# Where the D/2 row joins the first layer: VectorE's addition or ScalarE's write ahead of the products

## The chip, the cores and the metric

The kernel runs on one core of a Trainium2 chip. Its time is the device time of one launch in microseconds (us); the median of repeated runs is what is compared. Before the change it is 1832.67 us, the median of three runs (1832.33 to 1833.54).

## The reference

A two-dimensional Fourier transform of eight sequences, of which the real part is kept, followed by a hard-swish MLP on every token:

```
X = np.fft.fft(x, axis=1)             # x: (8, 3008, 256)
X = np.fft.fft(X, axis=2)
x = X.real.reshape(8 * 3008, 256)
h = x @ w_in                          # (256, 2048)
g = h * np.clip(h + 3.0, 0.0, 6.0) / 6.0
out = g @ w_out                       # (2048, 256)
```

## The kernel before

The transform along the sequence is done in two stages of matmuls (47 and 64 points) per pair of sequences; the transform along the 256 columns is folded into `w_in` once, which gives the table `W1`. What the first layer reads is `q`: the cosine half (block 0) and the sine half (block 1) of the columns, 128 rows each. The last row of block 1 isn't a sine: it is the column D/2. Its values, spread over all partitions, stand in `qn`, and its row of `W1`, turned into a column, in `WN`; so `qn * WN[:, f]` is what that row gives to 128 units of the hidden layer.

A *chunk* is 256 columns of `q` (one chunk in twelve, the last of a pair, has 194). There are 4 pairs of sequences, 12 chunks in a pair, and 8 steps (`fc`) in a chunk, each for 256 of the 2048 hidden units: 384 steps, `s`. From step 22 (`SPLIT`) on every step is one *cycle* of the main loop (L1394 on), which works on three chunks' steps at once:

- `odd_half` of step s+2: six TensorE products with the sine half (`half_products`, block 1) into the PSUM banks `u` and `v` in which the cosine half already lies; then ScalarE copies `v` to `y` (L669), VectorE joins it to `u` (L670), and ScalarE applies the first ReLU, `t<-u` (L708).
- `mlp2` of step s: seven products of the second layer (fourteen TensorE instructions, L758) into the four banks `acc`, from the gated values `a` and their sums `c`, which GpSimd makes (`combine`, L725).
- `even_half` of step s+3: six products with the cosine half (block 0) into the other pair of banks `u`, `v`. These six and the other six are in the split number format: three tables `KW[:, j]` by three parts `k[:, j]`, j = 0 and 1 into `u`, j = 2 into `v`.
- `add_row` of step s+3 (L653): two VectorE instructions, `d = qn * WN + v`. Then `keep_even` (L660), `s = u * (1 + EPS) + d`, the whole cosine half with the D/2 row.
- `other_sign` of step s+2 (L679), `v = u - 2 * s`, and its ReLU `t<-v`; then `first_gate` and `second_gate` (L711), which write `a`.

Both signs are needed, since a column and its mirrored one differ in the sign of the cosine half. In `odd_half` the last of the 128 rows of block 1 is the D/2 row, so that `u` takes it from the product there, and `s` takes it from `add_row`.

There are four such banks (`a0`, `a1`, `y0`, `y1`): the two of an even step and the two of an odd one. Some cycles *lend* them: where a stage of the transform of later data is due (`behind`, `middle_fns`), it takes the banks of step s+3 for itself after `mlp2`'s first product and before `even_half`; there `n` is 3, the order of the products is (0, 1, 2), and `add_row` and `keep_even` come after `first_gate`. In the other cycles `n` is 1: one second-layer product stands between `odd_half` and `even_half` and six behind it, and the order is (2, 0, 1), `v` first. In the last step of a chunk (`closes`) all of `mlp2` is issued before the rest, and ScalarE copies the four banks `acc` out to `e` (`copy_sums`, L775), two in that cycle, two in the next.

Every engine takes its instructions in the order in which the program issues them; the engines wait for each other through semaphores that the tile framework sets by the tiles that are read and written. The tiles `y`, `t` and `d` have one buffer each, `s` two.

Of the kernel before, what the change touches and what calls it, by code (L numbers as in the profile page):

```python
# [7 lines left out]
F32 = mybir.dt.float32  # L8
# [7 lines left out]
AF = mybir.ActivationFunctionType  # L16
# [44 lines left out]
def kernel(  # L61
# [10 lines left out]
    nc = tc.nc  # L72
    P = nc.NUM_PARTITIONS
# [16 lines left out]
    TB = KC * N2  # L90
# [20 lines left out]
    ps_u = ctx.enter_context(tc.tile_pool(name="ps_u", bufs=1, space=PSUM))  # L111
# [428 lines left out]
    class Chunk:  # L540
# [3 lines left out]
        def __init__(self, pr, ck):  # L544
            self.pr, self.ck = pr, ck
            self.last = ck == NCK - 1
            self.first = ck == 0 and pr.p == 0
            self.final = self.last and pr.p == NP - 1
            self.ns = 3 if self.last else KC
            self.n = self.ns * N2  # L550
            self.nq = P + 2 * NH if self.last else TB
            self.a, self.c, self.acc, self.front, self.k = {}, {}, {}, {}, None
            k1 = [(ck * KK + j // 2 + 1) % NK1 for j in range(KC)]
            b = [j % 2 for j in range(KC)]
            if pr.p == 0 and ck < 2 * NSG:
                k1 = [ck % NSG * KC + j + 1 for j in range(KC)]
                b = [ck // NSG] * KC
            self.blocks = [[(2 * b[j] + h, (k1[j], N1 - k1[j])[m]) for j in range(KC) for h in range(2)]
                           for m in range(2)]
            if self.last:  # L560
                for m in range(2):
                    self.blocks[m][4:] = [(m, 0), (2 + m, 0)]
# [68 lines left out]

        return others

    def half_products(ch, fc, blk, u, v, order=(2, 0, 1)):
        nq = ch.nq
        for j in order:
            for i in range(2):
                fs = slice((2 * fc + i) * P, (2 * fc + i + 1) * P)
                nc.tensor.matmul((u, u, v)[j][:, i, 0:nq], KW[:, j, blk, fs], ch.k[:, j, blk, 0:nq],  # L639
                                 start=(blk == i == 0 and j != 1), stop=True, skip_group_check=True)  # L640

    def even_half(ch, fc, step, order):
        u = ps_u.tile([P, 2, TB], F32, tag=f"a{step % 2}", name="u")
        v = ps_u.tile([P, 2, TB], F32, tag=f"y{step % 2}", name="v")
        half_products(ch, fc, 0, u, v, order)
        ch.front[fc] = [u, v]

    def add_row(ch, fc):
        of, nq, qn, (u, v) = ch.ck % 2 * TB, ch.nq, ch.pr.qn[ch.ck // 2], ch.front[fc]
        d = spool.tile([P, 2, TB], F32, tag="d", bufs=1, name="d")  # L650
        for i in range(2):
            f = 2 * fc + i
            nc.vector.scalar_tensor_tensor(d[:, i, 0:nq], qn[:, of:of + nq], WN[:, f:f + 1], v[:, i, 0:nq],  # L653
                                           op0=AL.mult, op1=AL.add)
        ch.front[fc].append(d)
# [4 lines left out]
        nc.vector.scalar_tensor_tensor(s[:, :, 0:nq], u[:, :, 0:nq], 1.0 + EPS, d[:, :, 0:nq], op0=AL.mult, op1=AL.add)  # L660
        ch.front[fc] = [u, v, s]

    def odd_half(ch, fc):
        nq, (u, v, s) = ch.nq, ch.front[fc]
        half_products(ch, fc, 1, u, v)
        y = spool.tile([P, 2, TB], F32, tag="y", bufs=1, name="y")
        t = spool.tile([P, 2, 2, TB], F32, tag="t", bufs=1, name="t")
        un, vn, yn, tn = u[:, :, 0:nq], v[:, :, 0:nq], y[:, :, 0:nq], t[:, :, :, 0:nq]
        nc.scalar.copy(yn, vn)  # L669
        nc.vector.scalar_tensor_tensor(un, un, 1.0 + EPS, yn, op0=AL.mult, op1=AL.add)  # L670
        copy_sums(1)
        relu(tn[:, 0], un, 1.0 / 6.0)
        copy_sums(1)
        ch.front[fc] = [u, v, t, s]
# [8 lines left out]
    def first_gate(ch, fc):  # L683
        u, v, t = ch.front[fc]
        a = apool.tile([P, 2, 2, TB], F32, tag="a", name="a")
        ch.a[fc] = a
        if not ch.last:
            gate(a[:, 0], t[:, 0], u[:])
            return
        gate(a[:, 0, :, 0:P], t[:, 0, :, 0:P], u[:, :, 0:P])  # L690
        for f in range(2):
            gate(slots(a[:, 0, f], N2 // 2, 1), *(slots(x, NH, 1)[:, :, 0:NH - 1] for x in (t[:, 0, f], u[:, f])))
# [492 lines left out]
    def chunk(s):  # L1185
        p, ck, fc = steps[s]
        return chunks[p][ck], fc
# [155 lines left out]
    for s, (p, ck, fc) in enumerate(steps):  # L1343
        now[0] = s
        if ck == 0 and fc == 0:
            ahead, behind, middle_fns = beside(p)
            if p + 1 < NP:
                feed.work.append(fold_pieces(pairs[p + 1]))
        t = ck * NF + fc
        if t == NST * (NG - 1) + 2:  # L1350
            assert not feed.work and not pieces, (s, len(feed.work), len(pieces))
        run(ahead, t)
        if s < NF:

            (second_steps if s % 2 else first_steps)(s)

            for part in LATER.get(s, ()):
                for dst, src in later[part]:
                    nc.sync.dma_start(out=dst, in_=src)
            run(middle_fns, t)  # L1360

        else:
            if pieces and pieces[0][0] <= s and t not in middle_fns and t not in behind:
                behind[t] = [(stage1, pieces.pop(0)[1:])]

            def sums():
# [12 lines left out]
                feed.cycle(cost, (4.75 if s < SPLIT else 4.44) + 0.9 * (t in middle_fns) + 1.2 * (t in behind))  # L1379

            if s < SPLIT:
                run(middle_fns, t)
                others = split_w(SPLIT_W.index(s)) if s in SPLIT_W else None
                activate(*chunk(s + 2), *mlp1_products(*chunk(s + 2)), between=others)
                sums()
                mlp2(*chunk(s), 0, 3)
                if s == SPLIT - 1:
                    even_half(*chunk(s + 3), s + 3, (2, 0, 1))
                    add_row(*chunk(s + 3))
                    keep_even(*chunk(s + 3))  # L1390
                stage1_parts(t)
                mlp2(*chunk(s), 3, 7)
                copy_sums(4)
            else:  # L1394
                turn_of[0] = s + 3
                borrows = t in behind or t in middle_fns
                n = 3 if borrows or s == SPLIT else 1
                odd, even = s + 2 < len(steps), s + 3 < len(steps)
                if s == SPLIT:
                    mlp2(*chunk(s), 0, n)  # L1400
                if odd:
                    odd_half(*chunk(s + 2))
                if s > SPLIT:
                    mlp2(*chunk(s), 0, 1)
                stage1_parts(t)
                run(middle_fns, t)
                if s > SPLIT and n > 1:
                    mlp2(*chunk(s), 1, n)
                if even:
                    even_half(*chunk(s + 3), s + 3, (0, 1, 2) if borrows else (2, 0, 1))  # L1410
                closes = fc == NF - 1
                if closes:
                    mlp2(*chunk(s), n, 7)
                    copy_sums(1)
                if even and not borrows:
                    add_row(*chunk(s + 3))
                if odd:
                    other_sign(*chunk(s + 2))
                if closes:
                    copy_sums(1)  # L1420
                if even and not borrows:
                    keep_even(*chunk(s + 3))
                if odd:
                    first_gate(*chunk(s + 2))
                if even and borrows:
                    add_row(*chunk(s + 3))
                    keep_even(*chunk(s + 3))
                if odd:
                    second_gate(*chunk(s + 2))
                sums()  # L1430
                if not closes:
                    mlp2(*chunk(s), n, 7)
                elif s + 1 == len(steps):
                    copy_sums(4)
        if fc == NF - 1:
            prev = chunks[p][ck]
# [102 lines left out]
```

## Time and profile before

| | |
|---|---|
| median of three runs | 1832.67 us |
| the profiled execution's own time | 1833.52 us |
| its span in the profile | 1831.7 us |
| granted TensorE clock | 0.997 |
| TensorE matmuls busy | 1816.0 us, 99% |
| VectorE busy | 1622.5 us, 89% |
| GpSimd busy | 1529.5 us, 83% |
| ScalarE busy | 962.7 us, 53% |

In the profile PE is TensorE, PEld its weight loads, DVE VectorE, ACT ScalarE, POOL GpSimd. A row of the timeline has the start of an instruction in us from the span's start, its duration, the engine, the line, the operation, the tile that it writes and those that it reads, and the shape; at its end, in brackets, the idle time of the engine before it and what ended it. Neighbouring instructions of one kind are merged (x4), and one in fp32 is two matmul instructions. Matmuls are pipelined: the start of one that follows another format is recorded before it streams, so that rates are read from start to start over a whole cycle.

### The profile page before, as it was taken

Reading aid. Unit: us, or ns where it says so; the run is one execution under the profiler, and the core shown is the slowest. Engines: PE = TensorE matmul, PEld = TensorE weight load, DVE = VectorE, ACT = ScalarE, POOL = GpSimd, SP = SyncE. Lnnn points to the kernel's source line nnn. Section 1 sums busy time; section 2 is a strip of 40 time slices with the busy share of each in tenths; the row PEclk is TensorE's granted clock in tenths of the full one; section 3 lists DMA queues with packets and bytes.
Section 4 is the critical chain, followed back from the end, with each engine's and each line's share of the span. In section 5 each row is a group of like instructions: output and inputs, shape, how many; then the busy total and the mean of one; then the engine's idle time right before and its main releaser. Section 6 shows DMA issues by size and latency. Waiting matters only on the chain.

```text
span 1831.7 us, 32501 instructions
## 1 busy us (share of the span) xinstructions
PE 1816.0 (99%) x10896; PEld 1620.8 (88%) x10896; DVE 1622.5 (89%) x3132; ACT 962.7 (53%) x1630; POOL 1529.5 (83%) x1694
## 2 busy tenths in 40 slices
PE   9999999999999999999999999999999999999997
PEld 6688888889998888899999888889999999999997
DVE  8978888888998888888998888888989989999897
ACT  6554555555455555554555555555554555555553
POOL 5687999998789999987778999998777778777884
PEclk9999999999999999999999999999999999999999
DMA  8433232321122313111122232310111111102001
GB/s 272 117 95 93 78 102 60 74 61 41 44 61 78 88 41 93 41 48 29 30 61 64 62 83 58 87 50 23 36 39 30 45 30 30 41 18 47 18 14 31
DMA packets 157629, 110.54 MB, mean 60 GB/s; under 512 B 121952, under 2 KB 136090, under 8 KB 157462
## 3 DMA queue, kind: packets, MB, share of 16 engines
q1 hardware_dynamic: 148710, 82.22, 18.0%
q0 software_dynamic: 7504, 25.65, 4.6%
q8 instruction: 87, 1.43, 0.3%
q10 hardware_dynamic: 1248, 0.59, 0.1%
q14 instruction: 80, 0.66, 0.1%
HBM read 71.93 MB, written 36.79 MB: 59 GB/s over the span
## 4 chain that ended last, share of the span: by engine, by line
PE 91%; DVE 5%; DMA 2%; ACT 1%; issue 1%; SPq 0%; ACTq 0%; DVEq 0%
PE acc L758 58%; PE u L639 18%; PE v L639 9%; PE ps L526 2%; PE ps L296 1%; DVE a L711 1%; PE v L577 1%; PE u L577 1%; PE acc L735 1%; DVE d L653 1%; DVE s L660 0%; DVE u L670 0%; DVE s L586 0%; ACT t L708 0%; DMA xt<-in_x_dram,IT 0%
## 5 line engine op out<-in xcount | busy, mean ns | idle before, releaser
L758 PE MATMUL acc<-c,G 128*128 128x256 f32 (+1 forms) x3008 | 697.4, 375 | 0.0
L758 PEld LDWEIGHTS acc<-c,G 128*128 128x128 f32 x3008 | 559.9, 190 | 70.1 <-POOL c L725 2.4
L758 PE MATMUL acc<-a,G 128*128 128x256 f32 (+1 forms) x2256 | 599.7, 376 | 0.0
L725 POOL TENSOR_TENSOR c<-a 128x512 f32<-128x512 f32 (+1 forms) x375 | 471.8, 1258 | 128.2 <-DVE a L711 111.7
L639 PE MATMUL u<-k,KW 128*128 128x256 f32 (+1 forms) x2880 | 468.6, 285 | 0.4 <-DVE s L660 0.2
L708 ACT ACTIVATE t<-u,half 128x512 f32<-128x512 f32 (+1 forms) x384 | 260.6, 679 | 309.1 <-DVE u L670 253.5
L758 PEld LDWEIGHTS acc<-a,G 128*128 128x128 f32 x2256 | 372.9, 189 | 37.3 <-issue 17.6
L639 PE MATMUL v<-k,KW 128*128 128x256 f32 (+1 forms) x1440 | 403.0, 361 | 0.7 <-DVE a L711 0.7
L639 PEld LDWEIGHTS u<-k,KW 128*128 128x128 f32 x2880 | 393.5, 189 | 5.9 <-ACT z L306 1.0
L669 ACT COPY y<-v 128x512 f32<-128x512 f32 (+1 forms) x360 | 207.7, 577 | 320.8 <-PE v L639 320.8
L708 ACT ACTIVATE t<-v,half 128x512 f32<-128x512 f32 (+1 forms) x384 | 260.3, 678 | 201.2 <-DVE v L679 200.5
L670 DVE SCALAR_TENSOR_TENSOR u<-u,y 128x512 f32<-128x512 f32 (+1 forms) x360 | 247.1, 686 | 110.5 <-ACT y L669 94.2
L653 DVE SCALAR_TENSOR_TENSOR d<-qn,WN,v 128x256 f32<-128x256 f32 (+1 forms) x720 | 307.2, 468 | 9.9 <-PE v L639 9.6
L639 PEld LDWEIGHTS v<-k,KW 128*128 128x128 f32 x1440 | 265.1, 189 | 35.9 <-PE u L639 1.5
L725 POOL TENSOR_TENSOR c<-a,c 128x256 f32<-128x256 f32 (+1 forms) x375 | 269.5, 719 | 29.4
L725 POOL TENSOR_TENSOR c<-c,a 128x256 f32<-128x256 f32 (+1 forms) x375 | 269.1, 718 | 29.4
L679 DVE SCALAR_TENSOR_TENSOR v<-s,u 128x512 f32<-128x512 f32 (+1 forms) x360 | 246.4, 684 | 51.9 <-ACT t L708 51.3
L711 DVE SCALAR_TENSOR_TENSOR a<-t,u 128x512 f32<-128x512 f32 (+2 forms) x448 | 260.4, 593 | 3.2 <-ACT t L708 3.2
L711 DVE SCALAR_TENSOR_TENSOR a<-t,v 128x512 f32<-128x512 f32 (+1 forms) x480 | 263.2, 565 | 0.1
L660 DVE SCALAR_TENSOR_TENSOR s<-u,d 128x512 f32<-128x512 f32 (+1 forms) x360 | 242.6, 674 | 2.5
L725 POOL TENSOR_TENSOR e<-e 128x512 f32<-128x512 f32 (+2 forms) x184 | 182.8, 994 | 0.0
L775 ACT ACTIVATE e<-acc 128x512 f32<-128x512 f32 (+2 forms) x184 | 98.6, 537 | 4.7 <-PE acc L758 4.2
(140 smaller groups left out, 1093.1 us busy)
## 6 DMA issues: line engine op xcount, KB each, us to landing
out_dram<-o SPq DMA_DIRECT2D x744, 32.0 KB
T<-in_c_stage_dram SPq DMA_DIRECT2D x26, 512.0 KB
g<-zd SPq DMA_DIRECT2D x42, 256.0 KB
zd<-z SPq DMA_DIRECT2D x48, 192.0 KB
xt<-in_x_dram SPq DMA_DIRECT2D x21, 256.0 KB
qn<-qd SPq DMA_DIRECT2D x16, 256.0 KB
st<-in_moe_w_out_dram POOLq DMA_DIRECT2D x7, 512.0 KB, 6.2
xt<-in_x_dram SPq DMA_DIRECT2D x17, 192.0 KB
```

What stands on the lines that cost most here:

```text
L526: nc.tensor.matmul(ps[:, blk, u * P:n].rearrange("p (b k) -> p b k", b=2), g[:, kk, blk * (P + 1):blk * (P + 1) + P], T[gr][:, :, blk, kk, ...
L639: nc.tensor.matmul((u, u, v)[j][:, i, 0:nq], KW[:, j, blk, fs], ch.k[:, j, blk, 0:nq], start=(blk == i == 0 and j != 1), stop=True, skip_g ...
L653: nc.vector.scalar_tensor_tensor(d[:, i, 0:nq], qn[:, of:of + nq], WN[:, f:f + 1], v[:, i, 0:nq], op0=AL.mult, op1=AL.add)
L660: nc.vector.scalar_tensor_tensor(s[:, :, 0:nq], u[:, :, 0:nq], 1.0 + EPS, d[:, :, 0:nq], op0=AL.mult, op1=AL.add)
L669: nc.scalar.copy(yn, vn)
L670: nc.vector.scalar_tensor_tensor(un, un, 1.0 + EPS, yn, op0=AL.mult, op1=AL.add)
L679: nc.vector.scalar_tensor_tensor(vn, sn, -2.0, un, op0=AL.mult, op1=AL.add)
L708: nc.scalar.activation(t, h, AF.Relu, bias=half[:], scale=scale)
L711: nc.vector.scalar_tensor_tensor(dst, t, 1.0, h, op0=AL.min, op1=AL.mult)
L725: (eng or nc.gpsimd).tensor_tensor(out, in0, in1, op=AL.add)
L758: nc.tensor.matmul(ch.acc[i // 2][:, i % 2, 0:ch.n], G[:, i, fc, :], mv, start=(fc == 0 and i % 2 == 0), stop=(fc == NF - 1), skip_group_c ...
L775: nc.scalar.mul(e, acc, 1.0 / WS)
```

## The change

In a cycle that lends no bank, and in which the bank's last user wrote its full width (`written`), ScalarE writes `qn * WN` into the bank `v` of step s+3 ahead of the cosine half's products (`seed_row`, two instructions behind the copy to `y`). The products for `v` then start without clearing the bank's marks, so that they add to what stands there, and come last (order (0, 1, 2)); three second-layer products stand ahead of them instead of one. `add_row` becomes a ScalarE copy of `v` to `d`, ahead of `other_sign`; `keep_even` moves behind `first_gate`. The products of the sine half take 127 rows in place of 128 for such a step, since `v` has the D/2 row already.

```diff
-    def half_products(ch, fc, blk, u, v, order=(2, 0, 1)):
+    def half_products(ch, fc, blk, u, v, order=(2, 0, 1), seeded=False):
...
-                nc.tensor.matmul((u, u, v)[j][:, i, 0:nq], KW[:, j, blk, fs], ch.k[:, j, blk, 0:nq],
-                                 start=(blk == i == 0 and j != 1), stop=True, skip_group_check=True)
+                nc.tensor.matmul((u, u, v)[j][:, i, 0:nq], KW[0:P - (blk and seeded), j, blk, fs],
+                                 ch.k[0:P - (blk and seeded), j, blk, 0:nq],
+                                 start=(blk == i == 0 and j == 0) or (blk == i == 0 and j == 2 and not seeded),
+                                 stop=True, skip_group_check=True)
...
+    def seed_row(ch, fc, step):
...
+        ch.front[fc] = [u, v]
+        of, nq, qn = ch.ck % 2 * TB, ch.nq, ch.pr.qn[ch.ck // 2]
+        for i in range(2):
+            f = 2 * fc + i
+            nc.scalar.activation(v[:, i, 0:nq], qn[:, of:of + nq], AF.Identity, scale=WN[:, f:f + 1])
...
+    def even_half(ch, fc, step, order):
+        seeded = fc in ch.front
+        if not seeded:
...
+            written[step % 2] = ch.nq == TB
+        half_products(ch, fc, 0, *ch.front[fc], order, seeded)
+        ch.seeded[fc] = seeded
...
     def add_row(ch, fc):
...
+        if ch.seeded[fc]:
+            nc.scalar.copy(d[:, :, 0:nq], v[:, :, 0:nq])
+            ch.front[fc].append(d)
+            return
...
-    def odd_half(ch, fc):
+    def odd_half(ch, fc, between=None):
...
-        half_products(ch, fc, 1, u, v)
+        half_products(ch, fc, 1, u, v, seeded=ch.seeded[fc])
...
         nc.scalar.copy(yn, vn)
+        if between:
+            between()
...
-                n = 3 if borrows or s == SPLIT else 1
                 odd, even = s + 2 < len(steps), s + 3 < len(steps)
+                seeds = even and not borrows and written.get(turn_of[0] % 2)
+                n = 3 if borrows or seeds or s == SPLIT else 1
...
+                if borrows:
+                    written[turn_of[0] % 2] = False
                 if odd:
-                    odd_half(*chunk(s + 2))
+                    odd_half(*chunk(s + 2), (lambda: seed_row(*chunk(s + 3), s + 3)) if seeds else None)
...
-                    even_half(*chunk(s + 3), s + 3, (0, 1, 2) if borrows else (2, 0, 1))
+                    even_half(*chunk(s + 3), s + 3, (0, 1, 2) if borrows or seeds else (2, 0, 1))
...
-                if even and not borrows:
+                if even and not borrows and not seeds:
                     keep_even(*chunk(s + 3))
                 if odd:
                     first_gate(*chunk(s + 2))
+                if even and seeds:
+                    keep_even(*chunk(s + 3))
```

More of the change, by code (lines that the diff above doesn't have):

```diff
@@ L551, in __init__ @@
             self.nq = P + 2 * NH if self.last else TB
-            self.a, self.c, self.acc, self.front, self.k = {}, {}, {}, {}, None
+            self.a, self.c, self.acc, self.front, self.seeded, self.k = {}, {}, {}, {}, {}, None
             k1 = [(ck * KK + j // 2 + 1) % NK1 for j in range(KC)]
@@ L638, in half_products @@
                 fs = slice((2 * fc + i) * P, (2 * fc + i + 1) * P)
-                nc.tensor.matmul((u, u, v)[j][:, i, 0:nq], KW[:, j, blk, fs], ch.k[:, j, blk, 0:nq],
-                                 start=(blk == i == 0 and j != 1), stop=True, skip_group_check=True)
-    def even_half(ch, fc, step, order):
+                nc.tensor.matmul((u, u, v)[j][:, i, 0:nq], KW[0:P - (blk and seeded), j, blk, fs],
+                                 ch.k[0:P - (blk and seeded), j, blk, 0:nq],
+                                 start=(blk == i == 0 and j == 0) or (blk == i == 0 and j == 2 and not seeded),
+                                 stop=True, skip_group_check=True)
+    written = {}
+    def seed_row(ch, fc, step):
         u = ps_u.tile([P, 2, TB], F32, tag=f"a{step % 2}", name="u")
         v = ps_u.tile([P, 2, TB], F32, tag=f"y{step % 2}", name="v")
-        half_products(ch, fc, 0, u, v, order)
         ch.front[fc] = [u, v]
+        of, nq, qn = ch.ck % 2 * TB, ch.nq, ch.pr.qn[ch.ck // 2]
[5 more added lines that the diff above has]
+        if not seeded:
+            u = ps_u.tile([P, 2, TB], F32, tag=f"a{step % 2}", name="u")
+            v = ps_u.tile([P, 2, TB], F32, tag=f"y{step % 2}", name="v")
+            ch.front[fc] = [u, v]
+            written[step % 2] = ch.nq == TB
+        half_products(ch, fc, 0, *ch.front[fc], order, seeded)
+        ch.seeded[fc] = seeded
     def add_row(ch, fc):
```

## The prediction

> **What bounds the kernel now.** I read the page first, then busy time by stretches, then the timeline of single cycles, then the groups by shape.
>
> ```profile
> span 1831.7 us, 32501 instructions
> PE 1816.0 (99%) x10896; PEld 1620.8 (88%) x10896; DVE 1622.5 (89%) x3132; ACT 962.7 (53%) x1630; POOL 1529.5 (83%) x1694
> ...
> PE 91%; DVE 5%; DMA 2%; ACT 1%; issue 1%; SPq 0%; ACTq 0%; DVEq 0%
> ...
> 600.00:900.00 300.00, 300.00 (x1800) 269.11 (x1799) 265.94 (x480) 159.33 (x269) 265.57 (x288) 1.00 0.22 55
> ```
>
> TensorE is busy all the time, and the chain of waits lies on it for 91%. The busy share alone proves little, since the ends of matmuls are modelled. So the question is whether a cycle lasts as long as its products stream, or longer. One full cycle that lends no bank, from the sine half's first product to the next one's:
>
> ```profile
> 903.51 0.59 PE L639 MATMUL v<-k,KW 128*128 128x256 f32 x2
> 904.19 0.59 ACT L669 COPY y<-v 128x512 f32<-128x512 f32 x1 [0.95 <-PE v L639]
> 904.65 0.59 PE L639 MATMUL v<-k,KW 128*128 128x256 f32 x2
> 904.81 0.70 DVE L670 SCALAR_TENSOR_TENSOR u<-u,y 128x512 f32<-128x512 f32 x1
> 905.42 0.86 DVE L653 SCALAR_TENSOR_TENSOR d<-qn,WN,v 128x256 f32<-128x256 f32 x2
> 905.54 0.69 ACT L708 ACTIVATE t<-u,half 128x512 f32<-128x512 f32 x1 [0.77 <-DVE u L670]
> 905.56 1.02 PE L758 MATMUL acc<-a,G 128*128 128x256 f32 x4
> 906.26 0.70 DVE L679 SCALAR_TENSOR_TENSOR v<-s,u 128x512 f32<-128x512 f32 x1
> 906.42 1.89 PE L758 MATMUL acc<-c,G 128*128 128x256 f32 x8
> 906.87 0.68 DVE L660 SCALAR_TENSOR_TENSOR s<-u,d 128x512 f32<-128x512 f32 x1
> 907.96 0.59 PE L639 MATMUL v<-k,KW 128*128 128x256 f32 x2
> 908.07 0.68 DVE L711 SCALAR_TENSOR_TENSOR a<-t,v 128x512 f32<-128x512 f32 x1
> 908.38 0.63 PE L639 MATMUL u<-k,KW 128*128 128x256 f32 x4
> ```
>
> The cycle takes 4.45 us, and its 26 matmul instructions have no gap. VectorE runs behind but in time: `s`, which the next sine half's products into `u` must find done, ends at 907.55, and those start at 908.38, 0.83 later. In these cycles the row's addition (0.86 us on VectorE) lies beside TensorE and costs nothing.
>
> Where there is something to gain is a pair's last chunk, whose products are shorter while VectorE's work shrinks less:
>
> ```profile
> 475.23 0.55 PE L639 MATMUL v<-k,KW 128*128 128x194 f32 x2
> 479.60 0.55 PE L639 MATMUL v<-k,KW 128*128 128x194 f32 x2
> ...
> 506.61 0.53 PE L639 MATMUL v<-k,KW 128*128 128x256 f32 x2
> 506.87 0.62 ACT L612 ACTIVATE k<-q 128x512 fp32r<-128x512 f32 x1
> 508.19 0.48 PE L639 MATMUL v<-k,KW 128*128 128x256 f32 x2 [0.23 <-DVE a L711]
> 510.79 0.53 PE L639 MATMUL v<-k,KW 128*128 128x256 f32 x2
> 515.49 0.59 PE L639 MATMUL v<-k,KW 128*128 128x256 f32 x2
> ...
> 1802.59 0.50 PE L639 MATMUL v<-k,KW 128*128 128x194 f32 x2
> 1806.20 0.50 PE L639 MATMUL v<-k,KW 128*128 128x194 f32 x2
> ```
>
> A cycle with everything short takes 3.61 us where nothing waits (1802.59 to 1806.20). With short halves and a full second layer it is 4.37 (475.23 to 479.60), so two full halves add 4.45 - 4.37 = 0.08 to a short one: 3.69. Nine cycles run from 479.60 to 515.49, 35.89 us. Streaming alone they would take five times 3.61, 0.89 for one that lends its banks (worked out below), 3.65 (half of the halves full) and twice 3.69 at the change to the next pair, and a full 4.45: 34.42. So 1.5 us are lost there to waits, in three pairs 4.5 us. The fourth pair's last chunk loses some 0.2. **About 4.7 us, 0.26%, is all that relieving VectorE can bring**, unless the streaming itself changes.
>
> **The change, part by part.** In the order of the changed program's instructions 281 of the 359 cosine halves in the main loop are seeded (261 full, 20 short); 68 cycles lend their banks and 10 follow one in a last chunk.
>
> *Streaming.* Twelve plus fourteen instructions as before. The new order, three second-layer products and then `u` before `v`, is the one that lending cycles have already:
>
> ```profile
> 543.03 0.58 PE L639 MATMUL v<-k,KW 128*128 128x256 f32 x2
> 544.36 1.05 PE L526 MATMUL ps<-T,g 128*128 128x128 f32 x8
> 545.65 0.58 ACT L529 COPY q<-ps 128x512 f32<-128x512 f32 x1
> 545.93 0.83 PE L639 MATMUL u<-k,KW 128*128 128x256 f32 x4
> 546.12 0.61 ACT L775 ACTIVATE e<-acc 128x512 f32<-128x512 f32 x1
> 546.59 0.40 PE L639 MATMUL v<-k,KW 128*128 128x256 f32 x2
> 548.37 0.58 PE L639 MATMUL v<-k,KW 128*128 128x256 f32 x2
> 549.04 0.58 ACT L669 COPY y<-v 128x512 f32<-128x512 f32 x1 [0.98 <-PE v L639]
> ```
>
> 543.03 to 548.37 is 5.34, 0.89 over a plain cycle, and the eight extra products account for it: they lie in a burst of 1.05 whose end overlaps what follows. The order costs nothing. The 127-row products are not in this trace in their format; the nearest are the first steps' fp32 ones:
>
> ```profile
> L577 PE MATMUL v<-q,W 127*128 127x256 f32 x96 | 25.4, 386 | 0.4 <-DVE a L711 0.2
> L577 PE MATMUL u<-q,W 128*128 128x256 f32 x96 | 24.7, 380 | 0.0
> ...
> L577 PEld LDWEIGHTS u<-q,W 128*128 128x128 f32 x96 | 18.0, 190 | 4.5 <-issue 1.9
> L577 PEld LDWEIGHTS v<-q,W 127*128 127x128 f32 x96 | 17.5, 189 | 5.0 <-DVE a L711 2.9
> ...
> L775 ACT ACTIVATE e<-acc 128x256 f32<-128x256 f32 x43 | 16.1, 376 | 0.0
> L429 ACT ACTIVATE zc<-z,FI 112x4 f32<-112x4 f32 x24 | 7.2, 300 | 0.8
> ```
>
> 386 against 380 ns bounds a product at 6 ns dearer; the weight loads, 189 against 190, bound the gain at 1 ns. I take 0: the 6 ns lie beside a wait for VectorE (0.4 us). For 281 x 6 products the ends are 10.1 us more and 1.7 us less.
>
> *ScalarE.* The two seeds aren't in the trace. Lower bound 376 ns, a write of the same size with a constant factor. Upper: a factor per partition costs 300 ns at 4 columns, 252 more at the slope of the ReLU at most (0.69 us for 512 columns, so under 1.35 ns each) come to 640. I take 450, nearer to the row of the same size. Neighbours on ScalarE start some 0.1 before the one ahead ends (545.65 + 0.58 against 546.12), so a pair takes about 0.8. The copy to `d` is the copy to `y` again, 0.59.
>
> The Trainium skill ("ScalarE: Activation LUTs", section "What ACT_TABLE_LOAD costs") gives an activation 186 ns and 0.833 ns a column, and 93 ns more for each factor held per partition. By it the seed is an estimated 492 ns, and a constant one 399, against the 376 measured here; the sum would be the same.
>
> *A full cycle after*, from the sine half's first product at 0: `y` 0.68 to 1.27; seeds 1.17 to about 1.97, once `second_gate` has left the bank (908.75, 0.79 into its cycle); `u` 1.30 to 2.00 and first ReLU 2.03 to 2.72 as before, so the seeds hide behind VectorE. Four second-layer instructions more, 0.86 (905.56 to 906.42), put the cosine half from 1.14 to 2.00, with `v` 0.66 behind that as in the lending cycle, at 2.66, and done at 3.06. The seeds are ready 0.7 before. VectorE: `v` sign 1.91 to 2.61, first gate 2.75 to 3.43. ScalarE: `d` 3.15 to 3.74, second ReLU, now queued behind it, 3.63 to 4.32. VectorE: `s` 3.77 to 4.45, second gate 4.37 to 5.05, which is 0.60 into the next cycle where it was 0.79. Next, TensorE needs `d` read by 4.45 (0.7 to spare) and `s` done by 4.87 (0.42 to spare, 0.83 before). **No new wait: 261 cycles x 0.**
>
> *Tightest place.* The first cycle of a chunk has two sums to copy on ScalarE as well. `y` at 0.67, seeds to 1.95, copy to 2.45, ReLU to 3.04, short copy (0.38) to 3.31, `d` to 3.80, `s` to 4.51: 0.30 of 4.81 remains. GpSimd gets `a` no later than before.
>
> *The last chunk.* `s` no longer waits for VectorE's two additions but for ScalarE's copy of a half that comes later. A second-layer instruction there is (4.37 - 3.61) / 14 = 54 ns shorter, so the cosine half begins at about 2.00 - 6 x 0.054 - 0.04 = 1.64 of 3.61 and `v` is done 1.06 later, at 2.70. With three quarters of the columns `d` takes some 0.48, to 3.27, and `s` 0.55, to 3.85; it is needed 0.36 after the cycle's end (4.81 less 4.45), at 3.97: none is lost, by 0.12. That recovers some 0.4 a pair. At the change of pairs (506.61 on) ScalarE has a split (0.62) ahead of `y`, then the seeds, a sum and `d`; `s` ends near 4.85 of a 3.69 cycle and the next products wait some 0.75. That is what these two cycles lose now (510.79 - 506.61 - 3.69 and 515.49 - 510.79 - 4.45 make 0.74). Nothing recovered.
>
> **The sum.** 1833.52 of the profiled execution, less 3 x 0.4 and 0.2: 1832.1. The median of the runs shown is 0.85 lower than that execution, so 1831.3 us, 0.08% less.
>
> **Rivals.** *All of the last chunk's waits go*: the change of pairs is VectorE's (0.23 <-DVE a), and VectorE has 0.86 less. Against it: ScalarE stands there with a split and two sums. It gives 1832.67 - 4.7 = 1828.0.
>
> *`s` comes late in a chunk's first cycle* (slower). For it: all the new work, the copy to `d` above all, stands on ScalarE between two copies of sums, and `s` behind it; against it, 0.30 in hand. From the point where seeds and copies take 0.30 longer than the rows say (a seed of 0.60), each 0.1 us costs 40 such cycles 4 us. At 0.2 beyond it: 8 us, 1839.3.
>
> *The 127-row products stream slower* (slower): for it the 386 against 380, against it the weight loads of 189 and 190. 1831.3 + 10.1 = 1841.4 at the bound.
>
> *The last chunk gives back what it gets*: `s` behind ScalarE's copy misses 3.97 by 0.1 to 0.2 in 20 cycles, which costs 2 to 4 us: 1833.3 to 1835.3.
>
> **How the numbers follow.** A measurement of this kernel can tell about 0.2%, 3.7 us, from no change. The forecast has 0.60 (1829 to 1834 by itself); all waits gone 0.12, of which 0.10 is under 1829.0; `s` late 0.11; slow products 0.11; given back 0.06. Faster 0.10, same 0.60 + 0.02 + 0.06 = 0.68, slower 0.22. The range goes from the ceiling of the gain, 1828, to the upper bound of the products, 1842: outside it lie the worse half of the late `s` and little else.
>
> **What would show it.** VectorE's busy time down by 261 x 0.86 + 20 x 0.73 = 239 us to about 1385; ScalarE's up by 281 x (0.8 + 0.59) = 390 to about 1350; TensorE's as it was. Full seeded cycles still 4.44 to 4.45 from sine half to sine half; `d` starting right behind `v`'s last cosine product, the second ReLU behind `d`, the second gate ending 0.6 into the next cycle. Wrong if a full seeded cycle takes 4.47 or more, if TensorE shows idle time released by ScalarE or by `s` (L660 of before), or if the last chunk's nine cycles take less than 34.7 or more than 36.5.

## The result and the profile after

The changed kernel takes 1852.99 us (median of five runs, 1852.22 to 1855.21), the kernel before on the same chip 1832.67 (five runs, 1832.1 to 1833.54). The ratio is 1.0111, with a 95% interval of 1.0099 to 1.0122: the change costs 20.3 us, 1.1%. Forecast were 1831.3, within 1828.0 to 1842.0, so the prediction was wrong, in sign and beyond its range. Of all the executions used below one, of run 5, took 6652.61 us for a reason that nothing here shows; the ratios leave it out.

The changed kernel's lines are numbered anew: the seeds are L654, the copy to `d` L670, `y` L691, `u` with `y` L694, `other_sign` L703, `s` L682, the ReLUs L732, the gates L735, the second layer L782, the copies of the sums L799. From the page of the profile after, busy times and groups:

```profile
span 1853.4 us, 32068 instructions
PE 1830.6 (99%) x10896; PEld 1628.9 (88%) x10896; DVE 1415.2 (76%) x2570; ACT 1315.6 (71%) x2473; POOL 1531.7 (83%) x1694
...
L703 DVE SCALAR_TENSOR_TENSOR v<-s,u 128x512 f32<-128x512 f32 (+1 forms) x360 | 246.6, 685 | 290.5 <-ACT t L732 290.4
...
L654 ACT ACTIVATE v<-qn,WN 128x256 f32<-128x256 f32 (+1 forms) x562 | 267.8, 476 | 13.2 <-DVE a L735 1.3
...
L670 ACT COPY d<-v 128x512 f32<-128x512 f32 (+1 forms) x281 | 163.0, 580 | 88.6 <-PE v L639 88.1
```

The work moved as forecast: 207 us less busy on VectorE, 353 more on ScalarE. TensorE is again "99% busy", and yet the span is 21.7 us longer. What is new stands in the idle columns and in the view of waits (engine, tile and line that waits, what it waits for; us in total, times, longest). Before:

```profile
DVE v L679 <- ACT t L708: 51.3, 69, 0.8
PEld u L639 <- DVE s L660: 0.8, 2, 0.4
PE u L639 <- DVE s L660: 0.2, 1, 0.2
```

and after:

```profile
DVE v L703 <- ACT t L732: 290.4, 350, 1.3
PEld u L639 <- DVE s L682: 17.5, 45, 0.7
PE u L639 <- DVE s L682: 5.7, 22, 0.5
```

The first row is VectorE's, which isn't the bound; its 290 us cost TensorE nothing by themselves. The other two are TensorE's: the sine half's products into `u` find `s` not done, 45 times in place of 2. The two rows overlap (a weight load and its product wait for the same thing), and the busy TensorE hides part of it. So I took the time from start to start of all 360 sine halves in both traces, cycle against cycle. The difference in the main loop falls into three parts:

| where | us |
|---|---|
| the 38 cycles that follow a chunk's first one, last chunks left out (the products waiting for its `s` lie there): 33 are longer by over 0.2, most of the plain ones 4.85 to 4.91 where they were 4.44 | 14.3 |
| the last chunk of each pair and the change to the next pair: 0.8 in each of three, 1.0 in the fourth | 3.4 |
| all other cycles; the full seeded ones, in the median, 4.447 where they were 4.439 | 1.8 |

(The profiled execution took 1855.21, 2.2 above the median. Ahead of step 22, where the change does nothing, its trace is 1.9 longer than that of the kernel before; the table leaves that out.)

**A plain seeded cycle.** The timeline of the kernel after, from the sine half's first product to the next:

```profile
908.31 0.59 PE L639 MATMUL v<-k,KW 127*128 127x256 f32 x2
909.56 0.70 DVE L694 SCALAR_TENSOR_TENSOR u<-u,y 128x512 f32<-128x512 f32 x1 [0.47 <-ACT y L691]
910.35 0.67 ACT L732 ACTIVATE t<-u,half 128x512 f32<-128x512 f32 x1
911.06 0.70 DVE L703 SCALAR_TENSOR_TENSOR v<-s,u 128x512 f32<-128x512 f32 x1 [0.80 <-ACT t L732]
911.42 0.59 ACT L670 COPY d<-v 128x512 f32<-128x512 f32 x1 [0.40 <-PE v L639]
911.66 0.68 DVE L735 SCALAR_TENSOR_TENSOR a<-t,u 128x512 f32<-128x512 f32 x1
912.26 0.68 DVE L682 SCALAR_TENSOR_TENSOR s<-u,d 128x512 f32<-128x512 f32 x1
912.76 0.59 PE L639 MATMUL v<-k,KW 127*128 127x256 f32 x2
```

VectorE stands still for 0.80 between `u` and `other_sign`, until the first ReLU has ended (910.35 + 0.67 = 911.02). My timetable had `other_sign` at 1.91 into the cycle; it starts at 2.75. `s` ends 4.63 into the cycle where the timetable had 4.45, with 4.87 as the time by which it is needed. The cycle still fits, with about 0.2 to spare instead of 0.42.

**A chunk's first cycle.** The same view where two copies of sums stand on ScalarE as well:

```profile
553.45 0.58 PE L639 MATMUL v<-k,KW 128*128 128x256 f32 x2
554.61 0.99 ACT L654 ACTIVATE v<-qn,WN 128x256 f32<-128x256 f32 x2
555.54 0.58 ACT L799 ACTIVATE e<-acc 128x512 f32<-128x512 f32 x1
556.01 0.68 ACT L732 ACTIVATE t<-u,half 128x512 f32<-128x512 f32 x1
556.73 0.70 DVE L703 SCALAR_TENSOR_TENSOR v<-s,u 128x512 f32<-128x512 f32 x1 [1.29 <-ACT t L732]
556.85 0.59 ACT L670 COPY d<-v 128x512 f32<-128x512 f32 x1
557.33 0.68 DVE L735 SCALAR_TENSOR_TENSOR a<-t,u 128x512 f32<-128x512 f32 x1
557.89 0.59 PE L639 MATMUL v<-k,KW 127*128 127x256 f32 x2
557.93 0.68 DVE L682 SCALAR_TENSOR_TENSOR s<-u,d 128x512 f32<-128x512 f32 x1
558.67 0.74 PE L639 MATMUL u<-k,KW 127*128 127x256 f32 x4 [0.19 <-DVE s L682]
562.79 0.59 PE L639 MATMUL v<-k,KW 127*128 127x256 f32 x2
```

Two seeds and a sum's copy push the end of the first ReLU back to 556.69, and `other_sign`, the first gate and `s` follow it one behind the other on VectorE. `d` is there at 557.44, but `s` starts at 557.93, because VectorE isn't free. It ends at 558.61. TensorE's `u` products, which follow `v`'s by 0.42 in the prediction's rows (907.96 to 908.38), start at 558.67, 0.78 behind 557.89. That cycle takes 4.90 (557.89 to 562.79) in place of 4.44.

**The last chunk.** The nine cycles that took 35.89 (479.60 to 515.49 in the prediction's rows) take 36.57 now, the bound of "wrong" having been 36.5. The first and last start, and what happens at the change of pairs:

```profile
483.89 0.44 PE L639 MATMUL v<-k,KW 127*128 127x194 f32 x1
...
514.40 0.69 DVE L703 SCALAR_TENSOR_TENSOR v<-s,u 128x512 f32<-128x512 f32 x1 [0.76 <-ACT t L732]
515.28 0.54 PE L639 MATMUL v<-k,KW 127*128 127x256 f32 x2
515.60 0.68 DVE L682 SCALAR_TENSOR_TENSOR s<-u,d 128x512 f32<-128x512 f32 x1
516.34 0.74 PE L639 MATMUL u<-k,KW 127*128 127x256 f32 x4 [0.52 <-DVE s L682]
520.46 0.47 PE L639 MATMUL v<-k,KW 127*128 127x256 f32 x1
```

### The profile page after: what moved, and what is told of

It is laid out like the page before. It is cut to its first block, busy times and chain, and to the rows that moved or that the text cites. A ratio compares the mean times of both kernels' runs of the same rounds, so it can differ in the third digit from the quotient of the medians.

```text
span 1853.4 us, 32068 instructions
## 1 busy us (share of the span) xinstructions
PE 1830.6 (99%) x10896; PEld 1628.9 (88%) x10896; DVE 1415.2 (76%) x2570; ACT 1315.6 (71%) x2473; POOL 1531.7 (83%) x1694
## 5 line engine op out<-in xcount | busy, mean ns | idle before, releaser
L782 PE MATMUL acc<-c,G 128*128 128x256 f32 (+1 forms) x3008 | 697.7, 375 | 0.0
L782 PEld LDWEIGHTS acc<-c,G 128*128 128x128 f32 x3008 | 539.8, 190 | 56.7 <-POOL c L749 2.4
L782 PE MATMUL acc<-a,G 128*128 128x256 f32 (+1 forms) x2256 | 554.2, 376 | 0.0
L639 PE MATMUL u<-k,KW 128*128 128x256 f32 (+3 forms) x2880 | 526.2, 304 | 8.4 <-DVE s L682 5.7
L703 DVE SCALAR_TENSOR_TENSOR v<-s,u 128x512 f32<-128x512 f32 (+1 forms) x360 | 246.6, 685 | 290.5 <-ACT t L732 290.4
L639 PEld LDWEIGHTS u<-k,KW 128*128 128x128 f32 (+1 forms) x2880 | 414.5, 189 | 36.4 <-DVE s L682 17.5
L782 PEld LDWEIGHTS acc<-a,G 128*128 128x128 f32 x2256 | 392.7, 190 | 51.7 <-issue 17.6
L691 ACT COPY y<-v 128x512 f32<-128x512 f32 (+1 forms) x360 | 207.8, 577 | 265.3 <-PE v L639 264.8
L639 PE MATMUL v<-k,KW 128*128 128x256 f32 (+3 forms) x1440 | 354.7, 328 | 0.0
L732 ACT ACTIVATE t<-u,half 128x512 f32<-128x512 f32 (+1 forms) x384 | 256.8, 669 | 118.9 <-DVE u L694 62.6
L694 DVE SCALAR_TENSOR_TENSOR u<-u,y 128x512 f32<-128x512 f32 (+1 forms) x360 | 247.3, 687 | 95.7 <-ACT y L691 64.5
L654 ACT ACTIVATE v<-qn,WN 128x256 f32<-128x256 f32 (+1 forms) x562 | 267.8, 476 | 13.2 <-DVE a L735 1.3
L732 ACT ACTIVATE t<-v,half 128x512 f32<-128x512 f32 (+1 forms) x384 | 261.9, 682 | 12.2 <-DVE v L703 11.6
L735 DVE SCALAR_TENSOR_TENSOR a<-t,u 128x512 f32<-128x512 f32 (+2 forms) x448 | 261.2, 595 | 3.3 <-ACT t L732 3.3
L639 PEld LDWEIGHTS v<-k,KW 128*128 128x128 f32 (+1 forms) x1440 | 247.4, 190 | 17.7 <-ACT v L654 0.6
L735 DVE SCALAR_TENSOR_TENSOR a<-t,v 128x512 f32<-128x512 f32 (+1 forms) x480 | 262.4, 563 | 0.1
L682 DVE SCALAR_TENSOR_TENSOR s<-u,d 128x512 f32<-128x512 f32 (+1 forms) x360 | 242.7, 674 | 2.5
L670 ACT COPY d<-v 128x512 f32<-128x512 f32 (+1 forms) x281 | 163.0, 580 | 88.6 <-PE v L639 88.1
```

Source lines behind the costliest of these rows:

```text
L639: nc.tensor.matmul((u, u, v)[j][:, i, 0:nq], KW[0:P - (blk and seeded), j, blk, fs], ch.k[0:P - (blk and seeded), j, blk, 0:nq], start=(bl ...
L654: nc.scalar.activation(v[:, i, 0:nq], qn[:, of:of + nq], AF.Identity, scale=WN[:, f:f + 1])
L670: nc.scalar.copy(d[:, :, 0:nq], v[:, :, 0:nq])
L703: nc.vector.scalar_tensor_tensor(vn, sn, -2.0, un, op0=AL.mult, op1=AL.add)
L732: nc.scalar.activation(t, h, AF.Relu, bias=half[:], scale=scale)
L735: nc.vector.scalar_tensor_tensor(dst, t, 1.0, h, op0=AL.min, op1=AL.mult)
```

## The experiments

Each ran beside the kernel before on one chip; the latter's median there is given as "before". "Seeded cycles" are those in which ScalarE writes the row. "Lost" is the difference from before, start to start, as in the table above.

**1. `s` ahead of the first gate.** The change, with `keep_even` back where it was:

```diff
-                if even and not borrows and not seeds:
+                if even and not borrows:
                     keep_even(*chunk(s + 3))
                 if odd:
                     first_gate(*chunk(s + 2))
-                if even and seeds:
-                    keep_even(*chunk(s + 3))
```

> The changed kernel with keep_even back ahead of first_gate in seeded cycles, as it stood before. Theory (ScalarE's queue): in a chunk's first cycle the seeds and a sum copy push the first ReLU to 2.56 us, other_sign on VectorE waits for that ReLU, and first_gate stands between other_sign and s, which ends at 5.16 instead of 4.8. With s ahead of the gate it can run at 4.02 to 4.70: the 0.4 us at the start of the second cycle of a chunk goes in all 41 chunks, and the time falls by 13 to 16 us to 1837 to 1840. Rival (127-row products stream slower): the order of VectorE changes nothing, 1850 to 1855. Rival (the copy to d itself is what is late): s waits for d as before, and less than 5 us are won.

1845.5 us (1844.86 to 1847.09; before 1833.35), ratio 1.0067 (1.0050 to 1.0084). Of the 14.3 lost in the cycles behind a chunk's first one, 4.0 are left, and TensorE's weight loads wait for `s` 7 times instead of 45. So `s` was late there because of what stood ahead of it on VectorE. It is more than the 1837 to 1840 expected. Both gates now end later, and in the next cycle the seeds wait for the bank that the second gate reads: 33 times, 10.1 us in all, where the change has 4 and 1.3. How much of the 4.0 this makes no run separates. From this kernel's timeline:

```profile
556.39 0.99 ACT L654 ACTIVATE v<-qn,WN 128x256 f32<-128x256 f32 x2 [0.25 <-DVE a L735]
```

The last chunks lose 4.9 where the change lost 3.4, and all other cycles 3.0 in place of 1.8. Neither place of `s` is free in this order.

**2. No seeds in a chunk's first cycle.**

```diff
-                seeds = even and not borrows and written.get(turn_of[0] % 2)
+                seeds = even and not borrows and fc > 0 and written.get(turn_of[0] % 2)
```

> The changed kernel, but a chunk's first cycle isn't seeded: there VectorE adds the row as before. Theory (ScalarE's queue in the first cycle): the 0.4 us at the start of the second cycle goes, 13 to 16 us of the 20, so 1836 to 1840; what the last chunks lose more stays. Rival (something that every seeded cycle pays): 36 to 40 of 281 seeded cycles less give 2 to 3 us, 1850.

1837.17 us (1836.43 to 1838.58; before 1833.35), ratio 1.0021 (1.0011 to 1.0030). As expected: what was lost behind a chunk's first cycle is gone (0.1 left in 38 cycles).

**3. The sums' copies behind the first ReLU**, in seeded cycles; the seeds stay everywhere:

```diff
-        copy_sums(1)
+        if not between:
+            copy_sums(1)
         relu(tn[:, 0], un, 1.0 / 6.0)
-        copy_sums(1)
+        copy_sums(2 if between else 1)
```

> The changed kernel, with both sum copies of the sine half behind the first ReLU instead of one ahead of it. Theory (the ReLU, and other_sign behind it, come late because of what ScalarE has ahead of the ReLU): the ReLU starts at about 2.1 instead of 2.56, s ends near 4.75 instead of 5.16, and nearly all of the 0.4 us goes: 1836 to 1841. Rival (the copy to d is what is late): that copy moves later by 0.1, nothing is won, 1852 to 1857.

1839.86 us (1839.35 to 1840.67; before 1833.35), ratio 1.0034 (1.0021 to 1.0047). As expected: the loss behind a chunk's first cycle falls from 14.3 to 0.4. Elsewhere outside the last chunks it is 3.3 in place of 1.8; nearly all of the difference lies in the chunks' first cycles, where weight loads of the second layer now wait for the later copies of the sums (19 times, 4.0 us). The waits of this kernel, in which the sums' copies take as long as ever and `d` still stands behind them:

```profile
DVE v L704 <- ACT t L733: 274.0, 350, 0.8
PEld u L639 <- DVE s L682: 4.8, 11, 0.7
```

`other_sign` waits as often as in the change (350 times), but for 0.8 at most instead of 1.3, and TensorE 11 times instead of 45. It is the *ReLU's* place on ScalarE that decides, by way of `other_sign`, not that of `d`.

**4. 127 rows alone.** The kernel before, with the sine half's products one row shorter; it leaves the D/2 row out of `u`:

```diff
-                nc.tensor.matmul((u, u, v)[j][:, i, 0:nq], KW[:, j, blk, fs], ch.k[:, j, blk, 0:nq],
+                nc.tensor.matmul((u, u, v)[j][:, i, 0:nq], KW[0:P - blk, j, blk, fs], ch.k[0:P - blk, j, blk, 0:nq],
```

> The kernel before, with 127 rows in the sine half's products in all 360 cycles; it leaves the D/2 row out of one half. Theory (a product costs its columns): within 2 us of 1832.7. Rival (127-row products stream slower by up to 6 ns): 360 x 6 x 6 ns, up to 13 us more, 1845.

1835.65 us (1835.18 to 1837.89; before 1833.35), ratio 1.0014 (1.0004 to 1.0023): 2.3 us, a little over the one expectation and far from the other. Fifteen cycles of the last pair, by the first and last start of a sine half, in the kernel before:

```profile
1724.38 0.58 PE L639 MATMUL v<-k,KW 128*128 128x256 f32 x2
...
1790.86 0.55 PE L639 MATMUL v<-k,KW 128*128 128x194 f32 x2
```

and in the experiment:

```profile
1725.78 0.47 PE L639 MATMUL v<-k,KW 127*128 127x256 f32 x1
...
1792.36 0.55 PE L639 MATMUL v<-k,KW 127*128 127x194 f32 x2
```

66.48 against 66.58 us: 6.7 ns a cycle, 1.1 ns for each of the six products. Over the change's 261 full seeded cycles that is 1.7 us, nearly all of the third part of the table. The rest of the trace agrees: outside the last chunks and the cycles behind a chunk's first one, the middle half of the cycles is 4 to 9 ns longer than before, and 4 to 10 ns in the change. A matmul's recorded duration can't show it; the start-to-start time over many cycles can. In cycles with 194 columns no difference is seen.

**5 and 6. Taking the ReLU and `other_sign` off the shared bank.** `u` joined with `y` is written over `y` in SBUF, and the ReLU, `other_sign` and the first gate read it there; once in the changed kernel, once in the kernel before as a control:

```diff
-        nc.vector.scalar_tensor_tensor(un, un, 1.0 + EPS, yn, op0=AL.mult, op1=AL.add)
+        nc.vector.scalar_tensor_tensor(yn, un, 1.0 + EPS, yn, op0=AL.mult, op1=AL.add)
...
-        relu(tn[:, 0], un, 1.0 / 6.0)
+        relu(tn[:, 0], yn, 1.0 / 6.0)
...
-        ch.front[fc] = [u, v, t, s]
+        ch.front[fc] = [y, v, t, s]
```

> The changed kernel, but VectorE writes the joined half over y in SBUF instead of over u in its bank; the first ReLU, other_sign and the gate read it there. other_sign then waits for no ReLU. Theory (s is late because other_sign waits for the ReLU that reads the same bank): in a chunk's first cycle other_sign runs at 2.0, first_gate at 3.3 to 4.0, s at 4.0 to 4.7; the stall of 0.4 us goes in all chunks, 1836 to 1840. Rival (ScalarE's own queue, the copy to d, is what is late): s waits for d as before, 1850 or more. Rival (an instruction on SBUF takes VectorE and GpSimd longer): over 1855.

> The kernel before with the same single change (the joined half in y). Theory: there the row's addition fills VectorE's time until the ReLU is done, so the wait costs nothing: within 2 us of 1833, at most 2 us won in the lending cycles and the last chunks. Rival (the wait for the ReLU costs in every cycle): 5 us or more won.

1997.41 us, ratio 1.0894 (1.0873 to 1.0916), and 1992.14, ratio 1.0867 (1.0849 to 1.0885), both against 1833.07. Both theories missed, by some 160 us; run 5's last rival, that an instruction on SBUF takes VectorE and GpSimd longer, is the one that fits. In one point the runs answer: in neither trace does `other_sign` wait for the ReLU any more, where it did so 350 times in the change and 69 times in the kernel before. In run 5 the two run side by side, though both read the one tile `y`:

```profile
1000.91 0.73 DVE L703 SCALAR_TENSOR_TENSOR v<-s,y 128x388 f32<-128x388 f32 x1
...
1000.99 0.60 ACT L732 ACTIVATE t<-y,half 128x388 f32<-128x388 f32 x1
```

So it is the shared bank that makes it wait, not the shared tile. But what that wait is worth can't be read here, since something else became dear. Groups by shape of run 6, where two of the three VectorE operations shown now have both inputs in SBUF:

```profile
L679 DVE SCALAR_TENSOR_TENSOR v<-s,y 128x512 f32<-128x512 f32 x328 | 371.5, 1133 | 2.1
L711 DVE SCALAR_TENSOR_TENSOR a<-t,y 128x512 f32<-128x512 f32 x328 | 298.8, 911 | 0.6
L711 DVE SCALAR_TENSOR_TENSOR a<-t,v 128x512 f32<-128x512 f32 x352 | 238.0, 676 | 0.0
...
L725 POOL TENSOR_TENSOR c<-c,a 128x256 f32<-128x256 f32 x344 | 331.7, 964 | 27.0
```

The second gate, whose `v` still lies in PSUM, is as fast as ever (676 ns); the first gate takes 911 against 678 in the kernel before, the sign 1133 against 696, and GpSimd's additions beside them 964 against 729. From the kernel before:

```profile
L679 DVE SCALAR_TENSOR_TENSOR v<-s,u 128x512 f32<-128x512 f32 x328 | 228.3, 696 | 47.2 <-ACT t L708 46.8
...
L725 POOL TENSOR_TENSOR c<-c,a 128x256 f32<-128x256 f32 x344 | 250.8, 729 | 27.0
```

**7. `s` behind the first gate, alone** (the kernel before; no seeds):

```diff
-                if even and not borrows:
-                    keep_even(*chunk(s + 3))
                 if odd:
                     first_gate(*chunk(s + 2))
+                if even and not borrows:
+                    keep_even(*chunk(s + 3))
```

> The kernel before, with keep_even behind first_gate in the cycles that lend no bank, nothing else. Theory (the move is harmless while the first ReLU is on time: s ends some 0.6 later, at 4.6 of 4.8): full cycles as before, last chunks 1 to 4 us worse, 1834 to 1838. Rival (the move alone makes s late in a chunk's first cycle): 1845 to 1850.

1835.87 us (1835.1 to 1836.87; before 1833.07), ratio 1.0016 (1.0006 to 1.0025). As expected: the move by itself loses nothing behind a chunk's first cycle (0.1 in 38 cycles). In the last chunks it loses 2.0, where the change lost 3.4. Elsewhere its trace is 1.3 longer, 1.2 of it in five single cycles of 0.2 to 0.3 each, while the median stays at 4.439; so much is the chance of one trace, and it isn't the few ns in every cycle of run 4.

**8. The order of the products alone** (the kernel before; three second-layer products ahead, `v` last, VectorE still adding):

```diff
-                n = 3 if borrows or s == SPLIT else 1
+                n = 3
...
-                    even_half(*chunk(s + 3), s + 3, (0, 1, 2) if borrows else (2, 0, 1))
+                    even_half(*chunk(s + 3), s + 3, (0, 1, 2))
```

> The kernel before, with three second-layer products ahead of the cosine half and u before v in every cycle, nothing else: VectorE's addition gets v some 1.4 us later in the cycle. Theory (s ends where VectorE's chain after v allows): d can't start before 3.1, s ends near 4.65 to 5.3 since d stands ahead of other_sign in VectorE's queue, so this order fits VectorE's addition badly: 1845 to 1900. Rival (the order costs nothing, as in the lending cycles): 1832 to 1835.

1985.4 us (1985.03 to 1986.46; before 1833.07), ratio 1.0831 (1.0812 to 1.0849), more than the 1845 to 1900 expected. Its waits:

```profile
DVE d L653 <- PE v L639: 270.5, 338, 1.3
...
PEld u L639 <- DVE s L660: 119.3, 283, 0.8
```

VectorE has `d` next in its queue when `v` comes late, and `other_sign` and `s` behind it wait too: the 152 us lost would be 0.45 for each of the 338 waits. So the order streams for nothing only as long as nobody early in a queue waits for `v`. The change could afford it since `d` went to ScalarE.

**9. `other_sign` issued ahead of the first ReLU**, in seeded cycles of the changed kernel:

```diff
         nc.vector.scalar_tensor_tensor(un, un, 1.0 + EPS, yn, op0=AL.mult, op1=AL.add)
+        if between:
+            nc.vector.scalar_tensor_tensor(vn, s[:, :, 0:nq], -2.0, un, op0=AL.mult, op1=AL.add)
+        ch.signed = bool(between)
```

> The changed kernel, but in seeded cycles VectorE's other_sign is issued ahead of ScalarE's first ReLU, so that it needn't wait until the ReLU has read bank u; now the ReLU waits for other_sign. Theory (s is late because other_sign waits for a late ReLU on the same bank): in a chunk's first cycle other_sign runs at 1.9 to 2.6, the ReLU at 2.63 to 3.31, first_gate ends at 4.0 and not 4.56, s at 4.7; the 0.4 us at the start of the second cycle goes, 1836 to 1840. Rival (ScalarE's queue alone, with the copy to d at its end): d is no earlier, the stall stays, 1850 or more.

1868.97 us (1868.05 to 1869.45; before 1832.8), ratio 1.0192 (1.0175 to 1.0209): missed, and slower than the change. ScalarE and VectorE in one plain cycle of it:

```profile
560.54 0.70 DVE L694 SCALAR_TENSOR_TENSOR u<-u,y 128x512 f32<-128x512 f32 x1 [0.31 <-ACT y L691]
561.27 0.69 DVE L696 SCALAR_TENSOR_TENSOR v<-s,u 128x512 f32<-128x512 f32 x1
562.85 0.69 DVE L739 SCALAR_TENSOR_TENSOR a<-t,u 128x512 f32<-128x512 f32 x1 [0.88 <-ACT t L736]
563.46 0.68 DVE L682 SCALAR_TENSOR_TENSOR s<-u,d 128x512 f32<-128x512 f32 x1
...
562.06 0.69 ACT L736 ACTIVATE t<-u,half 128x512 f32<-128x512 f32 x1 [0.68 <-DVE v L696]
```

Only the side that waits has changed: now the ReLU waits 0.68 for `other_sign`, and the gate 0.88 for the ReLU. From `u` to the start of `s` it is 2.92 here and 2.70 in the change. The loss behind a chunk's first cycle halves (7.4), but the median of the other cycles is 0.07 longer, 21.8 in all. Those 0.2 more on the chain are about what a plain cycle had left (0.24).

**10. Seeds only in a pair's first eleven chunks, and not in a chunk's first cycle.**

```diff
-                seeds = even and not borrows and written.get(turn_of[0] % 2)
+                seeds = even and not borrows and 0 < fc and not 85 <= s % 96 and written.get(turn_of[0] % 2)
```

> The changed kernel without seeds in a chunk's first cycle and without seeds in the last chunk's stretch (cycles 85 to 96 of a pair). Theory (three separate costs: the first cycles 15 us, the last chunks 3, the 127-row products 0.007 us in each full seeded cycle): the third alone is left, some 220 x 0.007, 1834 to 1836. Rival (something else that every seeded cycle pays): 1838 or more.

1835.2 us (1833.9 to 1837.46; before 1832.8), ratio 1.0011 (1.0001 to 1.0020). As expected: 2.4 us stay, 2.0 of them in the trace's main loop, none behind a chunk's first cycle and none in the last chunks: the few ns a cycle of run 4.

**11. The complement: seeds only in the last chunk and the cycle behind it.**

```diff
-                seeds = even and not borrows and written.get(turn_of[0] % 2)
+                seeds = even and not borrows and (85 <= s % 96 or s % 96 == 0) and written.get(turn_of[0] % 2)
```

> Seeds in the last chunk's stretch alone (cycles 85 to 96 of a pair), where VectorE's addition did cost something. Theory (there ScalarE's later copy to d gives back more than the addition took): 1834.5 to 1837, slower than the kernel before. Rival (the seeds do help where VectorE was late, and lose only elsewhere): 1829 to 1832.

1835.53 us (1835.34 to 1835.95; before 1832.8), ratio 1.0011 (1.0002 to 1.0021): 2.7 us lost, as expected; by the trace 3.3 in the last chunks, with the same loss in each pair as in the change, and nothing elsewhere.

The parts add up: 14.3 by the trace, 2.7 by run 11 and 2.4 by run 10 make 19.4 of the 20.3 us. (By run 2 the first part would be 20.3 - 3.8 = 16.5, and the sum 21.6; each median can be off by 1 to 2 us.) None of the versions is faster than the kernel before.

## Why the prediction was wrong

**The step that failed** is in the timetable of a full cycle: "VectorE: `v` sign 1.91 to 2.61, first gate 2.75 to 3.43". It lets `other_sign` run beside the first ReLU, as both only read `u`. They don't run side by side: `other_sign` starts when the ReLU has ended, 2.75 into the cycle. Runs 5 and 6 show that the shared bank is the reason (without it the wait is gone), and run 9 shows that one of the two waits in either order. The Trainium skill ("PSUM — Partial Sum Buffer", section "PSUM bank collisions raise a hardware error") says that two engines may not touch one bank's same partitions at one time, two readers included, and that software has to guard banks by semaphores; these waits agree with it, 0.80 in a plain cycle.

The trace of before had the evidence, and I passed over it. Its view of waits has the row `v` L679 for `t` L708 with 69 waits of up to 0.8; one of them, in a lending cycle, is `other_sign` at 545.79, in the timeline of the kernel before:

```profile
545.07 0.69 ACT L708 ACTIVATE t<-u,half 128x512 f32<-128x512 f32 x1 [0.77 <-DVE u L670]
...
545.79 0.70 DVE L679 SCALAR_TENSOR_TENSOR v<-s,u 128x512 f32<-128x512 f32 x1 [0.75 <-ACT t L708]
```

In the plain cycles, which I used for the timetable, no wait is printed, since VectorE was busy with the row's two additions in just that gap: `d` from 905.42 on, ReLU from 905.54 to 906.23, `other_sign` at 906.26, when both the ReLU and `d` had just ended. I read the 0.86 of the additions as work beside TensorE whose removal makes all that follows on VectorE earlier. In truth it filled a gap that stays: taking it away moved `other_sign` not at all (2.75 into the cycle before, 2.75 after).

**"Tightest place".** Named rightly, priced wrongly. I had `s` end at 4.51 of 4.81 by ScalarE's queue alone. With the sign behind the ReLU and the gate behind the sign, `s` ends 558.61 - 553.45 = 5.16 into the cycle. The price is in the first row of the table: 14.3 us. Not all of it is the missing wait's. In the kernel before, the next `u` products start 4.86 behind this cycle's start (548.37 to 553.23; my 4.81 was 0.05 early), so that `s` comes 0.30 late. Had the seeds taken the 0.8 I gave them, the ReLU would have ended at 3.04 and not at 3.24, and `s`, which ends 1.92 behind it, at an estimated 4.96: 0.10 late. The wait makes the place late, and the seeds' 0.19 more make it later; no run separates the two.

**The rival "`s` comes late in a chunk's first cycle"** (0.11, at 1839.3) was what happened, and it got the place and the count of cycles. Its condition, seeds and copies 0.30 dearer than the rows say, wasn't met: the pair of seeds takes 0.99 where I had 0.8, that is 0.19 more, and `d` ended at 3.99, which alone would have let `s` end by about 4.7 (in the same cycle of run 3 `d` ends at 3.99 too, and `s` at 4.72). What decided was the wait on VectorE, run 3 against the change: with `d` still behind both copies but the ReLU early, the loss is 0.4 us.

**The last chunk.** I had 0.4 recovered a pair, with `s` in time by 0.12, and at the change of pairs "Nothing recovered". Measured: a loss of 0.8 a pair, and 1.0 in the fourth. Single cycles there did become shorter, by up to 0.25, but those beside them lost more. Runs 10 and 11 show that the seeded cycles there cost it and nothing elsewhere does. The same wait of 0.76 stands in the row at 514.40, and `s` starts at 515.60 though `d` is long done; but run 7 loses 2.0 there with no seed at all, by the place of `s` alone, so how much is the wait's and how much the order's stays open. The rival "gives back what it gets" had 2 to 4 us for this, and 2.7 (run 11) to 3.4 were measured.

**The 127-row products.** "I take 0", between ends of 10.1 more and 1.7 less. Run 4 has 1.1 ns a product, 1.7 us for the change's 261 full cycles: near my value, on the dear side.

**What held.** The group of the row's additions on VectorE fell from 307.2 us (720 instructions) to 67.2 (158): 240, where 239 was forecast; the engine's busy time fell by only 207, as the rows of neighbours overlap and the overlap counts once. ScalarE got 267.8 + 163.0 = 431 us of instructions and 353 of busy time, 390 forecast. The copy to `d` starts 3.11 into a plain cycle (3.15 forecast). Most full seeded cycles stay at 4.45 and lose only the few ns of the 127 rows. "The order costs nothing" held with `d` off VectorE, and only so (run 8). The ceiling of the gain, 4.7 us, was never reached anywhere: even where the change had the most to win, in the last chunk, it lost.

## What to carry to other kernels

When work is taken off an engine, look for the wait that it was covering: an instruction that starts within a few hundredths of another engine's end (here `other_sign` at 906.26 behind the ReLU's 906.23) may be waiting for it, though the profile prints no wait while the engine is busy. In this kernel two engines that read the same PSUM bank belong one behind the other in a timetable, even when neither writes what the other reads. And put the whole queue of the cycle with the most extra work into that timetable before calling its slack enough: the price of being 0.3 us late there was paid in 33 cycles out of 360.

## What the runs showed of the hardware

- VectorE with both inputs in SBUF, beside a busy GpSimd: 1133 ns for a 128x512 operation that takes 696 with one input in PSUM, and GpSimd's 128x256 additions 964 against 729 (run 6). The 36 first gates of run 6 that had GpSimd beside them for less than half of their time took 674 to 680 ns, so that two inputs in SBUF alone aren't dear. The Trainium skill ("SBUF — State Buffer", section "Who interferes with whom") has VectorE contend with GpSimd for a shared port in just this case, two inputs in SBUF beside a GpSimd instruction that reads SBUF; the trace agrees, though it shows no port. Runs 5 and 6 lost some 160 us by it.
- A product with 127 rows in place of 128 is about 1.1 ns slower at 256 columns in the split format, start to start (run 4), and not measurably at 194.
- ScalarE's write of a seed into PSUM with a factor per partition takes 476 ns in the mean (L654, both widths), 0.99 for a full pair, where a write of 128x256 with a constant factor took 376 in the prediction's rows.
